# Mask through a product, exponential sums in PSUM and eight key blocks in a windowed attention kernel with two expert layers

## The chip, the cores and the metric

The kernel runs on one core of one Trainium2 chip. The core has TensorE (PE, with its weight loads shown apart as PEld), VectorE (DVE), ScalarE (ACT), GpSimd (POOL) and SyncE (SP), which here only issues DMAs. The metric is the device time of one execution in microseconds. Of the kernel before, three runs took 674.17, 674.81 and 678.31 us; their median is 674.81 us.

## The reference

There are three stages, all in float32.

- Attention: 4 batches, 8 heads, 512 local and 32 global tokens, head size 64. A local query sees the 32 global keys and the local keys at most 32 positions away (`mask = |i - j| <= 32`, else -1e9); a global query sees all 544 keys. Scores are scaled by 1/8; the softmax subtracts the row maximum and divides by (sum + 1e-9). This gives x of 2176 rows by 512.
- First layer: `h = x @ w_in` (512 to 1024); `solu = h * softmax(h)`; layer norm with `g_ln`; `@ w_out` (1024 to 512).
- Second layer: `h = x @ w_in` (512 to 2048); a piecewise square gate; `@ w_out` (2048 to 512).

The weights arrive as float64 and are converted on the chip to a high and a low float32 part.

## The kernel before

The local rows are cut into 16 tiles of 128 queries, four per batch, taken in the order SEQ = 0, 1, 3, 2, 4, 5, 7, 6 and so on; a number below is a place in this order. A tile has four chunks of 32 queries. Each chunk sees 128 keys: the chunk itself, one chunk on either side and the 32 global keys. So the scores of a tile are 8 heads by 128 keys for 128 partitions (4 heads by 32 queries), in two PSUM banks.

A step of a tile has a letter and its number t:

- q: the DMA of queries and keys (`load_qk`, `qkT`, two buffers); v: the DMA of the value windows (`load_vw`, `vw`, two buffers); w: the DMA of one of the first 16 pieces of the first layer's weights.
- S: 64 small products for the scores (L351), into one of two PSUM buffers of tag H, which the tiles of the first layer's `h` also use in turn. G: the products for the global queries (L404, L406); they read the same `qkT`.
- M: the mask on DVE (`mask`): an addition of `masks`, 128 x 512 values at the two edge blocks of every chunk, and, where a tile is the first or last of its batch, a memset of the missing block. R: the row maximum on DVE; Rn: its scaling.
- Ea, Eb: four exponentials each on ACT, one per head, with the row sum as accumulator output (L149, tile e). Ie: the addition of 1e-9 to the sums, on ACT where the list has a v behind it, else on DVE. I: their reciprocal on DVE.
- Ta, Tb: transposes on PE (`pPT`, L417); Pa, Pb: their copies to SBUF (`PT`). V: the products with the values (L432, tile o). X: their scaling on DVE (`xn`); XT: a transpose on DVE.
- A, C, B, D, F, H, L: the conversion of a weight piece (on DVE L173, L178, L180, L182, mostly).
- Z: three products with zeros (L276) that occupy PE in its first 20 us; ha to hB: the first layer's first product (L529); y, Y: its second (L270).

The order of all this is a written list, SCRIPT, whose 629 entries are issued one after the other; PE, SP, DVE, ACT and POOL keep its order on each engine. After it loops take over for the later tiles. A load waits on SP until its buffer is free, and all later loads wait behind it: q5 reuses the buffer of q3 and so waits for S3 and G3; v1 stands behind q5. The load w11 goes into the room of weight piece 3 and so waits for F3 on DVE; in SCRIPT F3 stands behind R5, D3 and X2, and on SP w14, q7, v4 and v5 stand behind w11.

The setup code (L125 to L130, L310) fills the identity, `masks` and `zero` on POOL and DVE. In DRAM, each tile's keys lie in 9 blocks of 32 (`KB`), where the blocks for global keys stand at 1, 4 and 7 (counted from 0), and a chunk's window starts at block 0, 2, 3 or 5 (`WSTART`).

Of the kernel before, what the change touches and what calls it, by code (L numbers as in the profile page):

```python
# [51 lines left out]
SCRIPT = """
Z0 q0 Z0 w0 qg0 S0 q1 w2 Z0 G0 w5 Gc0 S1 M0 A0v C0 R0 Rn0 B0 D0 F0 A2v Z0 G1 q2 M1 R1 C2 B2 D2 Ea0
A5 v0 Rn1 Z0 C5 B5 H0 Ta0 Eb0 F2 Ea1 Z0 Pa0 S2 Gc1 G2 Gc2 M2 Eb1 D5 H2 F5 R2 q3 L0v L2v Z0 Z0 G3
Gc3v Tb0 Ie0v w4 Rn2v I0 H5v Pb0 A4 C4 L5 V0 Ta1 Ea2 w1 S3 gm0 Pa1 A1v X0 Tb1 w7 Ie1v gn0 ge0 XT0 B4
q4 qg1 Eb2 xh0 C1 A7v gt0 B1 M3 C7 q5 xl0 D4 B7 Pb1 gp0 D1 R3 F1 D7 F4 v1 G4 n0 S4 w6 H4v M4 w3 Rn3v
Ie2v Ea3 Gc4 Ta2 Eb3 L4 V1 F7 H1 R4 I1 A6 Tb2 L1 H7 Pa2 S5 C6 Rn4v X1 v2 G5 Pb2 A3v L7 I2 XT1 q6 M5
B6 Ea4 Ta3 C3 B3 Gc5 Eb4 R5 V2 v3 Tb3 S6 Rn5v D3 Ie4v X2 Pa3 Pb3 F3 w9 D6 H3v w11 G6 Gc6v Ea5 M6
Ie3v Tb4 Eb5 F6 V3 I3 R6 w14 L3 XT2 A9v q7 H6 Ta4 X3 Pa4 L6 ha0 Rn6v v4 xh1 v5 A14 Ea6 C9 gi0 XT3 B9
hb0 Pb4 D9 hA0 Eb6 hB0 C14v B14 F9 G7 Ta5 Gc7 Tb5 V4 mx0 v6 D14 w8 ex0 F14 m9 Ie6v S7 ze0 I6 z0 I4  # L60
Pa5 u0 Pb5 M7 bn0v Ta6 xh2 pw0 X4 V5 Ie5v R7 Rn7v ha1 Ea7 gm1 Pa6 gn1 A11v XT4 Eb7 xl1 H9 Tb6 q8 I5
m14 C11 hb1 hA1 vn0 gc0 L9 w10 nn0v hB1 xl2v B11 ha2 xh3 D11 mx1 ta0 F11 X5 hb2 ex1 ge1 A8v hA2 hB2
H14v L14 ze1 tha0 z1 u1 tla0 Pb6 tb0 qg2 C8v m11 mx2 Ie7v V6 XT5 A10v bn1v thb0 gv0 pw1 S8 ex2 tlb0
X6 v7 go0 ze2v z2 u2 nn1v Ta7 w13 gt1 B8 Pa7 C10 I7 xh4 xl3 D8 ta1 gp1 B10 H11 F8 ha3 m8 L11 tha1 M8
v8 tb1 bn2v q9 Tb7 R8 thb1 H8 hb3 L8 hA3 Rn8v qg3 A13 D10 tlb1 w12 tla1 w15 Ea8 pw2 hB3 gc1 F10 XT6
mx3 s0 ya0 nn2 m10 Pb7 G8 Eb8 ex3 C13 B13 V7 Gc8 D13 X7 H10 ze3v G9 F13 z3 Gc9 S9 A12v Ie8v Ta8 L10
A15 u3 M9 bn3v R9 m13 xl4 C15 q10 Ya0 C12 tb2 B12 q11 ha4 s1 vn1 yca0 ta2 Pa8 hb4 Rn9 H13 thb2 hA4
D12 F12 Ea9 B15 m12 tha2 D15 hB4 tla2 tlb2 Tb8 F15 G10 L13 Eb9 A16 H12v Gc10v mx4 S10 I8 L12 M10 s2
Pb8 m15 G11 A17 XT7 v9 V8 pw3 Gc11 X8 v10 yb0 ex4 H15 ze4v C17 Ta9 L15v z4 Yb0 R10 Ie9v u4 xh5 nn3v
bn4v C16v I9 ycb0 Pa9v ta3 XT8 xl5 pw4 gm2 ha5 Rn10 tha3 tb3 hb5 nn4 B17 gi1 hA5 hB5 tla3 B16 Ea10  # L70
Eb10 thb3 Tb9 S11 xh6 Pb9 mx5 ex5 V9 ze5v tlb3 ta4 xh7 tha4v z5 u5 Ie10v A18 ya1 tb4 ha6 Ya1 v11 M11
bn5v hb6 X9 xl6v D16 D17 R11 F16 F17 hA6 gn2 yca1 Rn11 C18v H16v Ea11 tla4 Ta10 hB6 yb1 Eb11 thb4
tlb4 xh8v Tb10 q12 mx6 Pa10 B18 pw5 xl8 XT9 ge2 Pb10 I10 Ie11 D18 gv1 ex6 nn5v V10 ze6v X10 S12 Ta11
q13 z6 Yb1 M12 F18 go1 Pa11 u6 tb5 R12 ycb1 thb5v ha7 tlb5 gt2 L16 hb7 ta5 gp2 tha5 bn6 gc2 Tb11 I11
Rn12 xl7 pw6 H18v tla5 hB7 hA7 ya2 Ea12 nn6 Eb12 G12 Pb11v mx7 Gc12v S13 G13 ex7 gi2 Gc13v M13 Ie12v
v12 V11 q14 o0 tb6 thb6 L18 ze7 Ya2 ta6 z7 R13 Rn13v Ea13 Eb13 s3 xd0 u7 xd1 tlb6 XT10 H17v tha6
bn7v tla6 L17v Ie13 o1 X11 I12 I13 vn2 yca2 pw7 nn7 v13
"""
# [1203 lines left out]
```

## Time and profile before

| what | value |
|---|---|
| median of 3 runs | 674.81 us (674.17 to 678.31) |
| span of the profiled execution | 673.8 us; the page gives no other time for it |
| PE busy | 655.2 us (97%), 6089 instructions |
| PEld busy | 577.5 us (86%), 6092 |
| DVE busy | 432.9 us (64%) |
| ACT busy | 369.5 us (55%) |
| POOL busy | 259.8 us (39%) |
| DMA | 114.24 MB, 170 GB/s over the span |

A busy PE is not PE at its peak, because matmuls are pipelined and their ends are modelled. Idle time of an engine that nothing waits for costs nothing. In the page's 40 slices of 16.8 us each, PE's tenths are 7, 6, 8 and then 9 to the end but for the last slice.

### The profile page before, as it was taken

How to read it: one execution, taken by the hardware profiler on the slowest of the kernel's cores; microseconds unless marked ns; L12 is line 12 of the kernel's file. 1: busy time of each engine (PE TensorE's matmuls, PEld its weight loads, DVE VectorE, ACT ScalarE, POOL GpSimd, SP SyncE). 2: the span in 40 equal slices, each digit the busy share in tenths (PEclk: the TensorE clock that was granted, in tenths of full speed). 3: DMA queues.
4: the chain of work that ended last, by engine and by line, in shares of the span. 5: the costliest groups of instructions: out<-in, count | busy, mean ns of one | idle time of the engine just before them, and what ended most of it. 6: DMA issues, size and time to landing. Idle time of an engine off the chain costs nothing.

```text
span 673.8 us, 15103 instructions
## 1 busy us (share of the span) xinstructions
PE 655.2 (97%) x6089; PEld 577.5 (86%) x6092; DVE 432.9 (64%) x766; ACT 369.5 (55%) x918; POOL 259.8 (39%) x293
## 2 busy tenths in 40 slices
PE   7689999999999999999999999999999999999997
PEld 3467888989899889999999998998888888988986
DVE  5989987776787679654887679455655453333332
ACT  4888987556554244345666554554444466344443
POOL 2343463121112114203444676356776655222321
PEclk8979999999999999999999999999999999999999
DMA  8988854425752613301665341663333465744522
GB/s 321 358 348 333 343 203 159 165 65 164 288 193 92 254 32 125 95 1 32 187 188 186 128 125 63 217 220 126 125 126 125 134 210 190 237 136 157 170 81 80
DMA packets 29686, 114.24 MB, mean 170 GB/s; under 512 B 3376, under 2 KB 3888, under 8 KB 27056
## 3 DMA queue, kind: packets, MB, share of 16 engines
q1 hardware_dynamic: 29616, 113.28, 48.4%
q8 instruction: 48, 0.79, 0.5%
q14 instruction: 22, 0.18, 0.1%
HBM read 88.88 MB, written 24.38 MB: 168 GB/s over the span
## 4 chain that ended last, share of the span: by engine, by line
PE 90%; DMA 5%; DVE 3%; issue 1%; ACT 1%; SPq 0%; ACTq 0%
PE acc L270 26%; PE h L270 25%; PE yT L270 14%; PE h L529 13%; DMA vw<-in_vwin_dram 2%; PE plnT L594 2%; PE o L432 2%; DMA qkT<-in_qk_dram 2%; PE S L351 2%; PE pPT L417 2%; PE y L270 1%; PE og L492 1%; DVE xy L140 1%; PE G L404 0%; DVE w L180 0%
## 5 line engine op out<-in xcount | busy, mean ns | idle before, releaser
L270 PE MATMUL acc<-wo,g 128*128 128x512 f32 x816 | 211.3, 393 | 0.0
L270 PEld LDWEIGHTS acc<-wo,g 128*128 128x128 f32 x816 | 149.8, 188 | 23.2
L164 POOL TENSOR_TENSOR g<-xy,g 128x384 fp32r<-128x384 f32 (+1 forms) x65 | 62.8, 974 | 139.8 <-ACT g L149 122.4
L149 ACT ACTIVATE xy<-xy 128x384 f32<-128x384 f32 (+1 forms) x144 | 72.7, 505 | 71.5 <-DVE xy L140 68.5
L529 PE MATMUL h<-win,x 128*128 128x512 f32 x408 | 101.3, 400 | 0.0
L270 PE MATMUL yT<-lnT,wout 128*128 128x256 f32 x768 | 95.7, 284 | 0.0
L270 PEld LDWEIGHTS yT<-lnT,wout 128*128 128x128 f32 x768 | 93.4, 189 | 0.9
L529 PEld LDWEIGHTS h<-win,x 128*128 128x128 f32 x408 | 74.8, 188 | 15.9
L140 DVE TENSOR_TENSOR xy<-h,xy 128x384 f32<-128x384 f32 (+1 forms) x64 | 33.5, 524 | 62.1 <-PE h L270 60.9
L777 POOL TENSOR_TENSOR g<-xy,g 128x192 fp32r<-128x192 f32 x60 | 51.4, 876 | 54.2 <-ACT g L149 46.9
L149 ACT ACTIVATE g<-xy 128x384 fp32r<-128x384 f32 (+1 forms) x96 | 48.0, 500 | 18.7 <-DVE xy L140 16.7
L270 PE MATMUL h<-yT,w2i 128*128 128x384 f32 (+1 forms) x300 | 56.4, 334 | 0.0
L149 ACT ACTIVATE xy<-h 128x384 f32<-128x384 f32 (+1 forms) x64 | 30.0, 469 | 46.2 <-PE h L270 46.2
L270 PE MATMUL h<-yT,S 128*128 128x384 f32 (+1 forms) x288 | 54.9, 325 | 0.0
L270 PEld LDWEIGHTS h<-yT,w2i 128*128 128x128 f32 x300 | 52.5, 188 | 2.3
L140 DVE SCALAR_TENSOR_TENSOR xy<-h,xy 128x384 f32<-128x384 f32 (+1 forms) x48 | 26.1, 545 | 43.9 <-ACT xy L149 43.7
L270 PEld LDWEIGHTS h<-yT,S 128*128 128x128 f32 x288 | 48.8, 188 | 5.5 <-DVE xy L140 1.7
L149 ACT ACTIVATE e<-S,nm 128x128 f32<-128x128 f32 x128 | 45.3, 379 | 8.0 <-PE plnT L594 4.3
L571 POOL TENSOR_TENSOR rstd<-rstd,nhalf 128x1 f32<-128x1 f32 x17 | 11.4, 668 | 82.8 <-DVE rstd L140 49.6
L517 POOL TENSOR_TENSOR x<-xy,x 128x512 fp32r<-128x512 f32 x15 | 19.8, 1323 | 43.6 <-ACT x L149 35.5
L270 PE MATMUL h<-yT,lnT 128*128 128x384 f32 (+1 forms) x180 | 34.0, 334 | 0.1
L140 DVE SCALAR_TENSOR_TENSOR xy<-xy 128x384 f32<-128x384 f32 (+1 forms) x48 | 28.9, 602 | 7.8 <-ACT xy L149 7.8
(147 smaller groups left out, 1059.3 us busy)
## 6 DMA issues: line engine op xcount, KB each, us to landing
vw<-in_vwin_dram SPq DMA_DIRECT2D x16, 1024.0 KB, 7.0
wo<-w2d_o SPq DMA_DIRECT2D x32, 512.0 KB, 3.7
qkT<-in_qk_dram SPq DMA_DIRECT2D x15, 832.0 KB, 7.4
wraw<-in_w2i_dram SPq DMA_DIRECT2D x16, 512.0 KB, 3.7
wraw<-in_w2o_dram SPq DMA_DIRECT2D x16, 512.0 KB, 4.2
w2d_o<-wo SPq DMA_DIRECT2D x16, 512.0 KB, 5.1
w2d_s<-S SPq DMA_DIRECT2D x16, 512.0 KB, 5.5
S<-w2d_s SPq DMA_DIRECT2D x16, 512.0 KB, 5.9
```

The costliest lines, as they stand in the source:

```text
L140: self.last = getattr(nc.vector, name)(*args, **kw)
L149: vec.act = nc.scalar.activation(**kw)
L164: eng.tensor_tensor(out=lo, in0=src, in1=hi.bitcast(F32), op=ALU.subtract)
L270: mm(out=dst, lhsT=pairs[i][0][x], rhs=pairs[i][1][y], start=start and j == 0, stop=stop and j == 3 * n - 1, **kw)
L351: mm(out=S[32 * hp:32 * hp + 32, par, ci], lhsT=qT[r, hp, ci], rhs=kT[r, hp, w:w + 4].rearrange("p c d -> p (c d)"), start=True, stop=True)
L417: nc.tensor.transpose(ps[:, hp], eT[t][:, HP * par + hp], ident)
L432: mm(out=o[rows, ci, par], lhsT=PT[t][:, par, ci, rows], rhs=w[:, ci, D * h:D * h + D], start=True, stop=True)
L517: eng.tensor_tensor(out=xT[t][1], in0=x[:, :, n:n + P], in1=xT[t][0].bitcast(F32), op=ALU.subtract)
L529: mm(out=hps[t][:, half], lhsT=x[i][:, k], rhs=win[j][:, k, sl], start=not lo and j == 0 and k == 0, stop=lo and k == KD - 1)
L571: nc.gpsimd.tensor_tensor(sts[t].rstd, sts[t].rstd, nhalf, ALU.pow)
L594: nc.tensor.transpose(ps[:, k], ln[t][:, P * c:P * c + P], ident)
L777: eng.tensor_tensor(out=out, in0=x, in1=y, op=ALU.subtract)
```

## The change

The written list keeps its order but for two things: M1, M3 and M5 are gone, and each Ie stands directly behind the Eb of its tile instead of some way later.

- For tiles 0 to 5 the mask's addition on DVE is replaced by two products ahead of S, one for each PSUM bank: identity times a bfloat16 mask of 512 columns, with start and no stop, after which the 64 score products add to it. The memset of a missing block stays on DVE (tiles 0, 2 and 4).
- The accumulator output of an exponential goes to the first value of that head's scores in PSUM, which this exponential has read. Ie reads the eight sums there and writes them, with 1e-9 added, to SBUF. So the PSUM buffer is free only after Ie.
- Keys are stored in 8 blocks for 9: the global keys stand at blocks 2 and 5, the windows start at 0, 1, 3, 4. A load q has 768 KB for 832 KB. The windows keep the position of the masked blocks.
- Z reads 128 zeros four times for 512 zeros; POOL builds `maskb` and `identb` in the setup with a memset and five copies.

```diff
-WSTART = (0, 2, 3, 5)
-KB = 9
+WSTART = (0, 1, 3, 4)
+KB = 8
+MASKED = (0,1,2,3,4,5)
...
-            mm(out=ps, lhsT=zero[:, :P], rhs=zero, start=True, stop=True)
+            mm(out=ps, lhsT=zero, rhs=zero.unsqueeze(1).to_broadcast([P, 4, P]), start=True, stop=True)
...
-    zero = at1.tile([P, 512], BF16, name="zero")
+    zero = at1.tile([P, P], BF16, name="zero")
+    maskb = at1.tile([P, 4, 4, 32], BF16, name="maskb")
+    identb = at1.tile([P, P], BF16, name="identb")
...
+    nc.gpsimd.memset(maskb, 0.0)
+    nc.gpsimd.tensor_copy(identb, ident)
+    for c in range(4):
+        nc.gpsimd.tensor_copy(maskb[:, c, 0:4:3], masks)
...
+        own = t not in MASKED
+        for par in range(0 if own else 2):
+            mm(out=S[:, par].rearrange("p c n -> p (c n)"), lhsT=identb, rhs=maskb.rearrange("p c a n -> p (c a n)"), start=True, stop=False, skip_group_check=True)
...
-                       rhs=kT[r, hp, w:w + 4].rearrange("p c d -> p (c d)"), start=True, stop=True)
+                       rhs=kT[r, hp, w:w + 4].rearrange("p c d -> p (c d)"), start=own, stop=True, skip_group_check=not own)
...
-        tt(out=edge, in0=edge, in1=masks.unsqueeze(1).to_broadcast([P, H, 2, 32]), op=ALU.add)
+        if t not in MASKED:
+            tt(out=edge, in0=edge, in1=masks.unsqueeze(1).to_broadcast([P, H, 2, 32]), op=ALU.add)
...
-            act(out=eT[t][:, h], in_=heads(t)[:, h], func=AF.Exp, bias=nms[t][:, h:h + 1], scale=SCALE, accum_out=rs[t][:, h:h + 1])
+            act(out=eT[t][:, h], in_=heads(t)[:, h], func=AF.Exp, bias=nms[t][:, h:h + 1], scale=SCALE, accum_out=heads(t)[:, h, 0:1])
...
+    def sums_of(t):
+        return heads(t)[:, :, 0]
...
-        plus(rs[t])
+        plus(rs[t], of=sums_of(t))
...
-                        k = kT[r, hp, 2:8].rearrange("p (a c) d -> p a c d", a=2)[:, :, 0:2].rearrange("p a c d -> p a (c d)")
-                        mm(out=o[:, 32:32 + P].rearrange("p (a n) -> p a n", a=2), lhsT=lhsT, rhs=k, start=True, stop=True)
+                        k = kT[r, hp, 1:7].rearrange("p (a c) d -> p a c d", a=2)[:, :, 0:3:2]
+                        mm(out=o[:, 32:32 + P].rearrange("p (a c d) -> p a c d", a=2, c=2), lhsT=lhsT, rhs=k, start=True, stop=True)
...
-                plus(rs[i] if kind == "Ie" else sts[SEQ[i]].s, bool(v))
+                plus(rs[i] if kind == "Ie" else sts[SEQ[i]].s, bool(v), sums_of(i) if kind == "Ie" else None)
...
-        at = {0: -1, 2: 0, 3: 1, 5: 2, 6: 3, 8: 4}
+        at = {0: -1, 1: 0, 3: 1, 4: 2, 6: 3, 7: 4}
```

The weight step m also takes the engine that its caller names; in the list and the loops that is POOL, as before.

## Rows read from the trace of the kernel before

**Rows 1.** Stretch, length, busy PE, PEld, DVE, ACT, POOL (instructions), clock, DMA share, GB/s.
```profile
60.00:280.00 220.00, 219.88 (x2896) 196.35 (x2896) 173.81 (x321) 126.41 (x350) 64.99 (x61) 1.00 0.50 179
...
10.00:20.00 10.00, 8.61 (x177) 4.23 (x179) 8.66 (x16) 8.18 (x40) 1.23 (x2) 0.83 1.01 374
...
32.60:36.20 3.60, 1.11 (x62) 0.98 (x63) 3.10 (x6) 3.00 (x12) 2.87 (x3) 0.84 1.04 424
36.20:40.00 3.80, 3.80 (x95) 2.92 (x93) 2.29 (x5) 2.69 (x11) 2.12 (x3) 0.50 1.02 417
40.00:44.00 4.00, 4.00 (x145) 3.41 (x151) 4.00 (x8) 3.59 (x17) 0.00 (x0) 0.77 0.73 291
44.00:46.60 2.60, 2.39 (x100) 1.87 (x85) 2.51 (x7) 2.60 (x16) 1.29 (x1) 1.00 0.41 151
```

**Rows 2.** PE's waits from 0 to 80 us: total us, times, longest.
```profile
PE o L432 <- issue: 3.0, 2, 2.3
...
PE o L432 <- DMA vw<-in_vwin_dram: 1.5, 2, 0.8
```

**Rows 3.** Chain that ended last, 0 to 120 us: start us, us, what.
```profile
13.97 7.02 DMA qkT<-in_qk_dram
...
26.04 6.61 DMA vw<-in_vwin_dram
...
33.76 2.31 issue
...
42.78 0.60 DVE xn L140
43.38 0.61 DVE w L182
...
45.38 9.44 DMA vw<-in_vwin_dram
```

**Rows 4.** DMA issues, 0 to 60 us: count, KB each, median us to landing.
```profile
qkT<-in_qk_dram SPq DMA_DIRECT2D x8, 832.0 KB, 7.6
```

**Rows 5.** Timeline, POOL: start, us, instruction; and the costliest such group.
```profile
2.74 0.21 POOL L130 TENSOR_SCALAR_AFFINE_SELECT masks<-masks 32x32 f32<-32x32 f32 x1
...
masks.py:199 POOL TENSOR_SCALAR_AFFINE_SELECT ident<-ident 128x128 f32<-128x128 f32 x1 | 0.3, 293 | 0.0
```

**Rows 6.** Timeline, PE (Z at 15.26: first one, then all three).
```profile
10.42 1.44 PE L351 MATMUL S<-qkT 64*32 64x128 f32 x64 [1.52 <-DMA qkT<-in_qk_dram]
...
15.26 0.38 PE L276 MATMUL Z<-zero 128*128 128x512 bf16 x1
...
15.26 0.81 PE L276 MATMUL Z<-zero 128*128 128x512 bf16 x3
...
40.99 1.50 PE L432 MATMUL o<-vw,PT 128*32 128x64 f32 x64
...
54.96 1.10 PE L432 MATMUL o<-vw,PT 128*32 128x64 f32 x64 [0.83 <-DMA vw<-in_vwin_dram]
```

**Rows 7.** Timeline, DVE: start, us, instruction; in brackets the idle time before.
```profile
8.01 0.43 DVE L173 TENSOR_SCALAR w<-xy 128x512 int32<-128x512 int32 x1 [0.81 <-DMA xy<-in_w1i_dram]
...
36.69 0.69 DVE L140 TENSOR_TENSOR xn<-o,rs 128x512 f32<-128x512 f32 x1 [0.90 <-PE o L432]
...
39.69 0.70 DVE L140 TENSOR_TENSOR S<-S,masks 128x512 f32<-128x512 f32 x1 [1.02 <-PE S L351]
```

**Rows 8.** ACT groups, 0 to 60 us: count, busy us, mean ns, idle before.
```profile
L149 ACT ACTIVATE e<-S,nm 128x128 f32<-128x128 f32 x57 | 20.2, 376 | 0.7 <-DVE nm L140 0.4 <-DVE xn L140 0.3
L149 ACT ACTIVATION_READ_ACCUMULATOR e<-S,nm 128x1 f32 x56 | 12.1, 216 | 0.0
```

**Rows 9.** Stretches that end at the two stalls, and the page's instruction queue.
```profile
0.00:33.90 33.90, 23.88 (x601) 13.94 (x605) 25.48 (x48) 22.56 (x96) 9.86 (x25) 0.95 0.91 340
33.90:58.30 24.40, 20.97 (x509) 16.33 (x508) 22.26 (x45) 20.18 (x78) 8.05 (x9) 0.86 0.82 326
...
q8 instruction: 48, 0.79, 0.5%
```

More of the change, by code (lines that the diff above doesn't have):

```diff
@@ L50 @@
 SCRIPTED = 8
+MASKED = (0,1,2,3,4,5)
+PLAIN = ()
 SCRIPT = """
[L53 to L77, printed above, removed]
+Z0 q0 Z0 w0 qg0 S0 q1 w2 Z0 G0 w5 Gc0 S1 M0 A0v C0 R0 Rn0 B0 D0 F0 A2v Z0 G1 q2 R1 C2 B2 D2 Ea0
@@ new lines @@
+A5 v0 Rn1 Z0 C5 B5 H0 Ta0 Eb0 Ie0v F2 Ea1 Z0 Pa0 S2 Gc1 G2 Gc2 M2 Eb1 Ie1v D5 H2 F5 R2 q3 L0v
+L2v Z0 Z0 G3 Gc3v Tb0 w4 Rn2v I0 H5v Pb0 A4 C4 L5 V0 Ta1 Ea2 w1 S3 gm0 Pa1 A1v X0 Tb1 w7 gn0 ge0
+XT0 B4 q4 qg1 Eb2 Ie2v xh0 C1 A7v gt0 B1 C7 q5 xl0 D4 B7 Pb1 gp0 D1 R3 F1 D7 F4 v1 G4 n0 S4 w6
+H4v M4 w3 Rn3v Ea3 Gc4 Ta2 Eb3 Ie3v L4 V1 F7 H1 R4 I1 A6 Tb2 L1 H7 Pa2 S5 C6 Rn4v X1 v2 G5 Pb2
+A3v L7 I2 XT1 q6 B6 Ea4 Ta3 C3 B3 Gc5 Eb4 Ie4v R5 V2 v3 Tb3 S6 Rn5v D3 X2 Pa3 Pb3 F3 w9 D6 H3v
+w11 G6 Gc6v Ea5 M6 Tb4 Eb5 Ie5v F6 V3 I3 R6 w14 L3 XT2 A9v q7 H6 Ta4 X3 Pa4 L6 ha0 Rn6v v4 xh1
@@ new lines @@
+v5 A14 Ea6 C9 gi0 XT3 B9 hb0 Pb4 D9 hA0 Eb6 Ie6v hB0 C14v B14 F9 G7 Ta5 Gc7 Tb5 V4 mx0 v6 D14 w8
+ex0 F14 m9 S7 ze0 I6 z0 I4 Pa5 u0 Pb5 M7 bn0v Ta6 xh2 pw0 X4 V5 R7 Rn7v ha1 Ea7 gm1 Pa6 gn1 A11v
+XT4 Eb7 Ie7v xl1 H9 Tb6 q8 I5 m14 C11 hb1 hA1 vn0 gc0 L9 w10 nn0v hB1 xl2v B11 ha2 xh3 D11 mx1
+ta0 F11 X5 hb2 ex1 ge1 A8v hA2 hB2 H14v L14 ze1 tha0 z1 u1 tla0 Pb6 tb0 qg2 C8v m11 mx2 V6 XT5
+A10v bn1v thb0 gv0 pw1 S8 ex2 tlb0 X6 v7 go0 ze2v z2 u2 nn1v Ta7 w13 gt1 B8 Pa7 C10 I7 xh4 xl3
+D8 ta1 gp1 B10 H11 F8 ha3 m8 L11 tha1 M8 v8 tb1 bn2v q9 Tb7 R8 thb1 H8 hb3 L8 hA3 Rn8v qg3 A13
@@ new lines @@
+D10 tlb1 w12 tla1 w15 Ea8 pw2 hB3 gc1 F10 XT6 mx3 s0 ya0 nn2 m10 Pb7 G8 Eb8 Ie8v ex3 C13 B13 V7
+Gc8 D13 X7 H10 ze3v G9 F13 z3 Gc9 S9 A12v Ta8 L10 A15 u3 M9 bn3v R9 m13 xl4 C15 q10 Ya0 C12 tb2
+B12 q11 ha4 s1 vn1 yca0 ta2 Pa8 hb4 Rn9 H13 thb2 hA4 D12 F12 Ea9 B15 m12 tha2 D15 hB4 tla2 tlb2
+Tb8 F15 G10 L13 Eb9 Ie9v A16 H12v Gc10v mx4 S10 I8 L12 M10 s2 Pb8 m15 G11 A17 XT7 v9 V8 pw3 Gc11
+X8 v10 yb0 ex4 H15 ze4v C17 Ta9 L15v z4 Yb0 R10 u4 xh5 nn3v bn4v C16v I9 ycb0 Pa9v ta3 XT8 xl5
+pw4 gm2 ha5 Rn10 tha3 tb3 hb5 nn4 B17 gi1 hA5 hB5 tla3 B16 Ea10 Eb10 Ie10v thb3 Tb9 S11 xh6 Pb9
@@ new lines @@
+mx5 ex5 V9 ze5v tlb3 ta4 xh7 tha4v z5 u5 A18 ya1 tb4 ha6 Ya1 v11 M11 bn5v hb6 X9 xl6v D16 D17
+R11 F16 F17 hA6 gn2 yca1 Rn11 C18v H16v Ea11 tla4 Ta10 hB6 yb1 Eb11 Ie11 thb4 tlb4 xh8v Tb10 q12
+mx6 Pa10 B18 pw5 xl8 XT9 ge2 Pb10 I10 D18 gv1 ex6 nn5v V10 ze6v X10 S12 Ta11 q13 z6 Yb1 M12 F18
+go1 Pa11 u6 tb5 R12 ycb1 thb5v ha7 tlb5 gt2 L16 hb7 ta5 gp2 tha5 bn6 gc2 Tb11 I11 Rn12 xl7 pw6
+H18v tla5 hB7 hA7 ya2 Ea12 nn6 Eb12 Ie12v G12 Pb11v mx7 Gc12v S13 G13 ex7 gi2 Gc13v M13 v12 V11
+q14 o0 tb6 thb6 L18 ze7 Ya2 ta6 z7 R13 Rn13v Ea13 Eb13 Ie13 s3 xd0 u7 xd1 tlb6 XT10 H17v tha6
@@ L78 @@
+bn7v tla6 L17v o1 X11 I12 I13 vn2 yca2 pw7 nn7 v13
 """
@@ L183, in conv @@
         if step == "m" and w.scale is not None:
-            return nc.gpsimd.tensor_tensor(out=w.t3, in0=w.t3, in1=w.scale.unsqueeze(2).to_broadcast(list(w.t3.shape)), op=ALU.mult)
+            return eng.tensor_tensor(out=w.t3, in0=w.t3, in1=w.scale.unsqueeze(2).to_broadcast(list(w.t3.shape)), op=ALU.mult)
         if step == "H" and eng is nc.vector:
@@ L378, in exps, with plus @@
         for h in range(HP * half, HP * half + HP):
-            act(out=eT[t][:, h], in_=heads(t)[:, h], func=AF.Exp, bias=nms[t][:, h:h + 1], scale=SCALE, accum_out=rs[t][:, h:h + 1])
-    def plus(a, scalar=False):
+            act(out=eT[t][:, h], in_=heads(t)[:, h], func=AF.Exp, bias=nms[t][:, h:h + 1], scale=SCALE, accum_out=heads(t)[:, h, 0:1])
+    def plus(a, scalar=False, of=None):
         if scalar:
-            act(out=a, in_=a, func=AF.Copy, bias=EPS_SM)
+            act(out=a, in_=a if of is None else of, func=AF.Copy, bias=EPS_SM)
         else:
-            vec.tensor_scalar(a, a, EPS_SM, None, ALU.add)
+            vec.tensor_scalar(a, a if of is None else of, EPS_SM, None, ALU.add)
+    def sums_of(t):
+        return heads(t)[:, :, 0]
     def rsum(t):
-        plus(rs[t])
+        plus(rs[t], of=sums_of(t))
         vec.reciprocal(rs[t], rs[t])
```

## The prediction

> **What bounds the kernel now.** I read the busy time by stretch first. From 60 us to 280 us PE is busy for 219.88 of 220 us [rows 1], and the page's slices show it so to the end. What happens there on another engine is hidden as long as PE is fed, and the change adds nothing to PE there. So the change can move the end only by moving the moment, near 60 us, from which PE never waits again. All that follows is about the first 60 us.
>
> There the waits of PE come next [rows 2], then the chain of waits [rows 3]. The chain runs from load to load: q3 (issued 13.97, 7.02 us), then S3 frees the buffer for q5, and v1 behind it lands after 6.61 us; V1 stops in its middle for 2.31 us with no releaser ("issue"); then S5, R5, X2 and F3 on DVE let SP issue w11, w14, q7 and v4, and v4 takes 9.44 us from its issue at 45.38. V4 starts at 54.96 when it has landed [rows 6]. DVE is busy nearly throughout, yet it waits 0.90 us for V1 at X1 and 1.02 us for S5 at M5 [rows 7]: it isn't the chain by itself. DMA has share 1.01 to 1.04 between 10 and 20 us and between 32.6 and 40 us, and 0.73 and 0.41 after that [rows 1].
>
> **The change, part by part.** The sum is made against the profiled execution: span 673.8 us, 1.0 us under the median of the runs, 674.8; I add that 1.0 at the end.
>
> *Loads q.* Each has 64 KB less of 832 KB [rows 4]. By the time q3 lands, q0 to q3 have moved 256 KB less; at 374 GB/s [rows 1], with DMA full, that is 0.70 us. q5 saves 64 KB before v1, at 424 GB/s 0.15 us; q7 the same before v4. I take -0.70, -0.15 and -0.15; the bounds are 0 (if something other than bytes sets the landing) and these values.
>
> *Mask products.* The nearest row is Z, the same shape: three take 0.81 us at clock 1.00 [rows 6]. Two thirds of it, 0.54, is the upper bound; the first alone lasts 0.38, so each further one adds (0.81-0.38)/2 = 0.215, and a pair in a stream adds 0.43. I take 0.43, as S follows at once. Where the clock is 0.50 (1.2 GHz) I double it: 0.86. Tile by tile:
> - S0 also waits for POOL, whose last select ends at 2.95; six small operations of at most 0.293 us [rows 5] end by 4.7. With 0.43 and some 1.5 us for 64 products S0 ends by 6.7, and R0 stands behind a DVE conversion that starts at 8.01 when its weights land [rows 7]. Cost 0; cover left 1.3.
> - S1: PE waits 1.52 us for q1 [rows 6], and the two products need no keys. Cost 0. S2: it delays G2 and so q4 by up to 0.43, but q4 isn't on the chain. Cost 0.
> - S3 is on the chain: +0.43. S4 is followed by a wait of PE for v1 of 0.7 us (1.5 in two waits, the longer 0.8) [rows 2]. Cost 0.
> - S5 lies between 36.2 and 40 us, where the clock was 0.50 throughout, after PE had been busy 1.11 of 3.60 us [rows 1]: +0.86; lower bound 0.43.
>
> *Mask additions.* Six of 0.70 us [rows 7] leave DVE, 4.2 us. M0's and M1's room goes into waits for loads and S1. M2 to M4 are 2.1 us before X1, where DVE waits for V1 anyway: it waits longer. M5's goes into the wait for S5. So 0 on the chain, and what is late next is V1, S5, V2. If DVE were the chain, it would be up to -2.1; that is a rival.
>
> *Sums into PSUM.* The trace has no ACT output into PSUM. An exponential and its accumulator read last 376 and 216 ns [rows 8] and overlap. For the read into PSUM I bound the difference by half its duration either way, 0.1 us, so 0.8 us in eight; I take 0, the value of the row it is nearest to, the same read into SBUF. The last tile of the opening whose buffer PE then needs at once is 5; there up to 0.8 us would delay ha, and behind it PE has 0.83 us of wait before V4 [rows 6] as cover. The Trainium skill ("ScalarE: Activation LUTs", "What happens when an `exp` ACTIVATE runs") calls PSUM the lower-latency destination for ScalarE. By that the difference is a gain, and no run here shows it; the sum stays the same, as the cover stands at the same place.
>
> *Ie.* It now stands on ACT before what followed Eb, and holds the PSUM buffer for about 0.22 us more (the accumulator read, 0.216, is the nearest row). For ha, which takes tile 5's buffer, this is +0.22 on PE, before the same cover. Ie11 and Ie13 stand on DVE and wait there for ACT; behind them are conversions of a stretch in which DVE is busy 79% [rows 1] and PE needs nothing at once. Cost 0.
>
> *Z, the pattern of G, smaller `zero`.* The number of columns is the same. Cost 0.
>
> **The sum.** V1: -0.70 + 0.43 - 0.15 = -0.42. V2: -0.42 + 0.86 = +0.44. V2 ended at 40.99 + 1.50 = 42.49; now 42.93. X2 started at 42.78 [rows 3] behind D3, which comes earlier by M5's room; so X2 now waits for V2 and starts 0.15 later; F3 and w11 too. q7 gives back 0.15. v4 lands at the same time as before: 0.00. PE reaches V4 0.44 + 0.22 = 0.66 later than it did, within its 0.83. So the time is 673.8 + 0.0 + 1.0 = 674.8 us: no change that can be measured. Its own range, from the bounds, is 673.9 (mask of S5 at full clock and V2 no gate) to 675.8 (no gain from bytes); with the sums at their upper bound V4 would be 0.66 + 0.8 - 0.83 = 0.6 late, which lies within it.
>
> **The stall inside V1.** The term that I put at 0 and am least sure of. 1206 matmul and load records come before it and 1017 lie between it and the second one, of 0.7 us, in V5 [rows 9, 2]. TensorE's queue fetched 48 pieces in 0.79 MB [rows 9], 16 KB each; 12,181 PE and PEld instructions over 48 are 254, and 1017 is four times 254. So both stalls look like the ends of fetched pieces, with DMA full around the first [rows 1]. By V1 the change has put 20 instructions (four for each of S0 to S4) ahead: the piece now ends 20 instructions sooner in V1, still there. I take the same stall. The Trainium skill ("Runtime: NRT & Kernel Launch", "Instruction fetch mechanics") says that crossing a block is mostly hidden. By that rule the 2.31 us would not be there; the trace disagrees at two of the nine or so pieces in 60 us, so it can vanish as well as grow.
>
> **Rivals.**
> - *The fetch meets a pause of PE and the stall goes* (chance 18%). 2.31 us less for V1; S5 then runs at full clock, and DVE has its 2.1 us. What is late next is DMA: between 40 and 46.6 us it is idle for (1-0.73)*4.0 + (1-0.41)*2.6 = 2.6 us [rows 1], and the loads up to v4 can't come earlier than that. 674.8 - 2.6 = 672.2; with the second stall gone too 671.5. For it: seven pieces ended without a stall. Against: V1 is the densest run of instructions.
> - *DVE was the chain* (12%): the M2 to M4 part passes through, 674.8 - 2.1 = 672.7. For it: DVE busy 4.00 of 4.00 us before F3 [rows 1]. Against: its waits at X1 and M5 [rows 7].
> - *Slower: the bytes give nothing and the products cost* (16%). If the landings don't follow the bytes, S3 and S5 remain: V2 ends at 42.49 + 1.29 = 43.78, X2, F3 and v4 are 1.00 later: 675.8. It decides from the point where q3 takes more than 6.8 us from issue to landing.
> - *The stall grows or a third one comes* (8%): another 2.31 us in the densest part, with DMA full: 677.1.
> - *The sums or Z don't do what is written*: the read takes as long into PSUM, Z's repeated zeros run like plain ones. Both are my zeros already, so this is part of the forecast.
>
> My forecast has 40%; 6% are left to what the trace doesn't hint at, half of it on either side and over 1%.
>
> **How the numbers follow.** Predicted is the forecast's 674.8. Range 671.3 to 677.3: it takes in all four rivals and leaves out the last 6% and a part of the bounds. 1% is 6.7 us, about what a measurement of this kernel can tell from no change; none of the cases reaches it, up to 58 us PE is idle for 10.0 + 3.4 us in all [rows 9], half of which would have to go, so faster by over 1% gets 0.05, slower 0.05, within 0.90.
>
> **What would show it.** In the profile after: DMA of q3 at about 6.5 us from its issue; pairs of mask products of 0.43 us before S3 and up to 0.86 before S5; no DVE addition on S before tile 6; X1 waiting longer than 0.90 us for V1; a stall of some 2 us in V1, about ten products sooner; V4 starting within 1 us of 54.96. Wrong it would be if V4 starts 2 us earlier with the stall gone, if PE waits for ACT's Ie ahead of an S or ha after 60 us, or if PE isn't full after 60 us.

## The result: slower, outside the range, and the profile after

The changed kernel takes 681.56 us (median of four runs, 680.47 to 683.34) against 674.97 for the kernel before in the same comparison: the medians are 6.6 us apart. The ratio is 1.0088, with a 95% interval of 1.0061 to 1.0115; it is formed from the single runs of a comparison and isn't the quotient of the medians (of 675 us it is 5.9). The range ended at 677.3. The profiled execution of the changed kernel is the slowest of its four; its span is 681.3 us, before's was 673.8, so the two traces are 7.5 us apart.

One row holds most of it. The waits of PE in the changed kernel, over the whole span (total us, times, longest):

```profile
PE h L545 <- DVE rs L143: 4.0, 1, 4.0
...
PE G L420 <- issue: 1.8, 1, 1.8
...
PE o L448 <- issue: 0.9, 2, 0.6
```

The first row wasn't there before: PE waited 4.0 us for `rs` on DVE, in a part of the span where I had said it never waits. The timeline of PE in the changed kernel shows where (start, us, instruction; in brackets the idle time before and its releaser):

```profile
161.07 0.60 PE L610 MATMUL plnT<-ident,e 128*128 128x128 f32 x4
165.68 7.40 PE L545 MATMUL h<-win,x 128*128 128x512 f32 x24 [4.01 <-DVE rs L143]
```

It is the first product of the first layer for one tile, 24 products. Before, the same rows were:

```profile
159.40 0.60 PE L594 MATMUL plnT<-ident,e 128*128 128x128 f32 x4
159.76 5.85 PE L529 MATMUL h<-win,x 128*128 128x512 f32 x24
```

So 1.67 us of the 7.5 had come up by `plnT`, and 5.80 came at this one h: it starts 4.25 later against `plnT`, and its 24 products take 7.40 for 5.85, 1.55 more. The other executions below say which of the two parts is the change. From the start of this `plnT` to the end of its span before's takes 514.4 us (673.8 less 159.40). The ten others in which PE doesn't wait at this h take 513.9 to 515.3; the changed kernel takes 520.2, 5.8 more than before's. The start of `plnT` scatters: e1, e8 and e8b run the same steps as the changed kernel up to there, and have it at 158.85, 159.07 and 160.14, where the changed kernel has 161.07 and before's 159.40. So the 5.80 at h is the change, and the 1.67 is no more than that scatter.

What DVE did at that place in the changed kernel:

```profile
157.96 1.21 DVE L143 TENSOR_REDUCE nm<-S 128x8 f32<-128x1024 f32 x1
165.45 0.17 DVE L143 TENSOR_SCALAR rs<-S 128x8 f32<-128x8 f32 x1 [6.29 <-ACT e L152]
...
165.76 1.24 DVE L143 SCALAR_TENSOR_TENSOR e<-e,s,h 128x1024 f32<-128x1024 f32 x1
```

The second row is Ie13. It stands 6.29 us, idle, until ScalarE has finished the last tile's exponentials. Behind it in DVE's order stands u7 (the last row, `hmul`), which reads the h of the tile before and so frees its PSUM buffer. In the kernel before, u7 ran early and Ie13 (`rs`) late:

```profile
157.63 1.24 DVE L140 SCALAR_TENSOR_TENSOR e<-e,s,h 128x1024 f32<-128x1024 f32 x1
...
164.74 0.17 DVE L140 TENSOR_SCALAR rs<-rs 128x8 f32<-128x8 f32 x1
```

The two buffers of tag H are held by that h, until u7, and by the scores S13, until Ie13 has read the sums in them. Both now end at or behind Ie13, and the next h starts at 165.68, when Ie13 has run.

The starts also tell which buffer it takes. Before, h starts at 159.76, behind u7 and ahead of S13's exponentials (from 160.10): it has the buffer that u7 freed. In the changed kernel it starts ahead of u7 (165.76), released by Ie13: it has S13's own. The built programs say the same. That choice isn't the cost: u7 now ends at 167.00, so the other buffer would have come later still.

Ahead of this stands ScalarE. Its timeline in the changed kernel, from the first to the last of the eight exponentials of S13:

```profile
161.76 0.37 ACT L152 ACTIVATE e<-S,nm 128x128 f32<-128x128 f32 x1 [2.36 <-PE plnT L610]
162.03 0.16 ACT L152 ACTIVATION_READ_ACCUMULATOR e<-S,nm 128x1 f32 x1
...
165.26 0.16 ACT L152 ACTIVATION_READ_ACCUMULATOR e<-S,nm 128x1 f32 x1
```

The first of them starts when PE has done `plnT` (161.67), which reads a tile e; the trace names it as the releaser. So PE's last product ends, ScalarE then runs eight exponentials, DVE Ie13, and only then PE goes on.

The pitch of these exponentials is the second finding. Before, in the timeline of ScalarE, one started every 0.345 us:

```profile
10.17 0.36 ACT L149 ACTIVATE e<-S,nm 128x128 f32<-128x128 f32 x1
10.42 0.20 ACT L149 ACTIVATION_READ_ACCUMULATOR e<-S,nm 128x1 f32 x1
10.52 0.36 ACT L149 ACTIVATE e<-S,nm 128x128 f32<-128x128 f32 x1
```

and in the changed kernel every 0.46 us:

```profile
11.12 0.37 ACT L152 ACTIVATE e<-S,nm 128x128 f32<-128x128 f32 x1
11.39 0.16 ACT L152 ACTIVATION_READ_ACCUMULATOR e<-S,nm 128x1 f32 x1
11.58 0.37 ACT L152 ACTIVATE e<-S,nm 128x128 f32<-128x128 f32 x1
```

Each instruction by itself became shorter. The groups of ScalarE from 0 to 60 us in the changed kernel (count, busy us, mean ns) answer to [rows 8]:

```profile
L152 ACT ACTIVATE e<-S,nm 128x128 f32<-128x128 f32 x56 | 20.6, 367 | 1.4
L152 ACT ACTIVATION_READ_ACCUMULATOR e<-S,nm 128x1 f32 x56 | 9.3, 166 | 0.0
```

The read takes 166 ns for 216. But the next exponential used to start 0.10 after the read had begun, beside it; now it starts 0.19 after, when the read is over. A group's mean can't show that; the starts do.

Last, the clock. Stretches of the changed kernel (length; busy PE, PEld, DVE, ACT, POOL with instructions; granted clock, DMA share, GB/s):

```profile
161.70:165.70 4.00, 0.03 (x1) 0.03 (x1) 0.25 (x2) 3.71 (x17) 0.00 (x0) 1.00 0.24 66
165.70:173.00 7.30, 7.30 (x25) 5.81 (x26) 6.31 (x14) 2.37 (x6) 0.55 (x1) 0.77 0.43 136
...
167.70:168.70 1.00, 1.00 (x4) 0.81 (x3) 1.00 (x4) 0.97 (x4) 0.00 (x0) 0.50 0.00 0
```

PE was busy 0.03 of 4.00 us. In the stretch behind that the mean granted clock is 0.77; from 166.7 to 169.7 it is 0.50, which is 1.2 GHz, as in the last row. Three us at half speed cost about 1.5 (an estimate from these rows), which is the 1.55 us.

### The profile page after: what moved, and what is told of

It reads as the page before. It is cut to its first block, busy times and chain, and to the rows that moved or that the text cites. A ratio compares the mean times of both kernels' runs of the same rounds, so it can differ in the third digit from the quotient of the medians.

```text
span 681.3 us, 15118 instructions
## 1 busy us (share of the span) xinstructions
PE 661.2 (97%) x6099; PEld 580.7 (85%) x6104; DVE 427.2 (63%) x760; ACT 376.1 (55%) x918; POOL 261.5 (38%) x299
## 4 chain that ended last, share of the span: by engine, by line
PE 91%; ACT 4%; DVE 3%; issue 1%; POOL 0%; POOLq 0%; ACTq 0%
PE acc L273 26%; PE h L273 25%; PE h L545 14%; PE yT L273 13%; PE o L448 2%; PE plnT L610 2%; PE S L363 2%; ACT e L152 2%; PE pPT L433 2%; PE y L273 1%; PE og L508 1%; PE G L420 1%; DVE xy L143 1%; ACT Sg L152 0%; PE pg L488 0%
## 5 line engine op out<-in xcount | busy, mean ns | idle before, releaser
L545 PE MATMUL h<-win,x 128*128 128x512 f32 x408 | 103.0, 405 | 4.0 <-DVE rs L143 4.0
L545 PEld LDWEIGHTS h<-win,x 128*128 128x128 f32 x408 | 76.2, 192 | 20.5 <-DVE rs L143 4.2
L152 ACT ACTIVATE e<-S,nm 128x128 f32<-128x128 f32 x128 | 47.0, 368 | 10.2 <-PE plnT L610 3.8
L273 PEld LDWEIGHTS h<-yT,lnT 128*128 128x128 f32 x180 | 31.6, 188 | 2.0 <-DVE xy L143 0.5
```

The costliest lines, as they stand in the source:

```text
L152: vec.act = nc.scalar.activation(**kw)
L273: mm(out=dst, lhsT=pairs[i][0][x], rhs=pairs[i][1][y], start=start and j == 0, stop=stop and j == 3 * n - 1, **kw)
L545: mm(out=hps[t][:, half], lhsT=x[i][:, k], rhs=win[j][:, k, sl], start=not lo and j == 0 and k == 0, stop=lo and k == KD - 1)
```

## The experiments

The theory after the two traces: Ie13's place on DVE costs most of it, the sums in PSUM some, and the mask products with the eight blocks nothing. The rivals: the mask products or blocks are what costs; h waits for S13's own buffer, wherever Ie13 stands.

| kernel | median us | ratio to before (95%) |
|---|---|---|
| changed | 681.56 | 1.0088 (1.0061 to 1.0115) |
| e1 Ie13 on ScalarE | 677.45 | 1.0031 (1.0016 to 1.0045) |
| e2 sums in SBUF | 679.61 | 1.0077 (1.0059 to 1.0094) |
| e3 mask products and blocks alone | 674.27 | 1.0001 (0.9981 to 1.0022) |
| e4 before, Ie13 moved | 680.07 | 1.0077 (1.0047 to 1.0107) |
| e5 blocks alone | 674.88 | 0.9987 (0.9975 to 0.9999) |
| e6 mask products alone | 675.92 | 1.0007 (0.9994 to 1.0021) |
| e7 sums in the other bank | 676.06 | 1.0024 (1.0003 to 1.0044) |
| e8 Ie13 behind u7 | 676.23 | 1.0007 (0.9995 to 1.0020) |
| e8b the same again | 676.19 | 1.0018 (1.0002 to 1.0034) |
| e9 e8, sums in SBUF | 675.41 | 1.0009 (0.9992 to 1.0026) |
| e10 sums alternating | 677.25 | one run |
| e11 sums without own wait | 675.79 | 1.0021 (1.0005 to 1.0037) |

Before's median was 674.84 beside e1 to e4, 675.43 beside e5 to e8, 675.18 beside e8b to e10 and 674.71 beside e11; ratios, not times, are compared across these groups. A ratio of 0.001 is 0.7 us.

**e1, Ie13 on ScalarE** (the changed kernel):

```diff
- ... Eb13 Ie13 s3 xd0 u7 xd1 ...
+ ... Eb13 Ie13v s3 xd0 u7 xd1 ...
```

> The changed kernel with one entry different: Ie13 runs on ACT and no longer on DVE. Theory A (two costs: DVE stands at Ie13 for 6.3 us, so u7 behind it frees no buffer and TensorE idles 4.0 us and then runs 1.5 us longer at the lower clock; the rest, 1.7 us, comes from the exponentials before 60 us): the wait of 4.0 us is gone, 681.6 - 5.8 = 675.8 us, with TensorE still about 1.7 us late at 60 us. Theory B (it is the PSUM buffer of tile 13 that is held longer, whichever engine adds): the wait stays, 681 us.

The wait is gone: `plnT` at 158.85 is followed by h at 159.20. The ratio falls from 1.0088 to 1.0031, so theory A holds for the larger part. It missed the rest: 677.45 is 1.7 us over what it gave, and PE isn't 1.7 us late near 60 us, as V4 starts at 55.03, where before's started at 54.96. Where the remaining 0.0031 (2.1 us) goes isn't shown.

**e2, sums in SBUF** (the changed kernel, Ie where the change put it, now adding in place):

```diff
- accum_out=heads(t)[:, h, 0:1]
+ accum_out=rs[t][:, h:h + 1]
```

> The changed kernel with the exponentials' sums going to SBUF again and Ie adding in place; list, mask products and eight blocks stay. Theory A: an exponential with its accumulator read is back from a pitch of 0.46 to 0.345 us, TensorE reaches its last wait near 60 us some 1.7 us earlier, and the exponentials of tile 13 end 0.9 us earlier, so the wait at Ie13 is 3.1 instead of 4.0 us: 679.0 us. Theory C (the mask products or the loads cost the 1.7 us): pitch back, but the opening as slow: 680.7 us.

The waits of PE:

```profile
PE h L545 <- ACT e L152: 3.1, 1, 3.1
```

The same h still waits, now 3.1 us and for the last exponential itself, as S13's buffer is then free when Eb13 ends. 4.01 - 3.06 = 0.95, and eight exponentials at 0.115 more make 0.92: that much of the wait was the pitch. The time, 679.61, lies between theory A's 679.0 and theory C's 680.7 and doesn't decide between them; e3 does.

**e3, mask products and blocks alone** (sums in SBUF, every Ie in its place of before):

> Mask products and eight key blocks alone: sums in SBUF and every Ie where the kernel before has it. Theory A: neither cost is left, 674 to 675 us, at most 1 us from the kernel before. Theory C: 676.5 us.

1.0001 (0.9981 to 1.0022): these two parts together cost nothing that can be measured, with about 1.4 us of room either way. The rival falls.

**e4, only Ie13 moved** (the kernel before, otherwise untouched):

```diff
- ... Eb13 s3 xd0 u7 xd1 ... L17v Ie13 o1 ...
+ ... Eb13 Ie13 s3 xd0 u7 xd1 ... L17v o1 ...
```

> The kernel before with one entry moved: Ie13, on DVE and with sums in SBUF, directly behind Eb13. Theory A: DVE waits there for ACT, u7 is late, TensorE idles about 3.1 us and runs on at the lower clock for a while: 675.0 + 4.5 = 679.5 us. Theory B: sums in SBUF hold no PSUM buffer, so 675.0 us.

One word of the list makes the kernel before 1.0077 times as long, 5.2 us (3.2 to 7.2). Its timeline of DVE:

```profile
161.69 0.17 DVE L140 TENSOR_SCALAR rs<-rs 128x8 f32<-128x8 f32 x1 [5.54 <-ACT e L149]
...
162.00 1.24 DVE L140 SCALAR_TENSOR_TENSOR e<-e,s,h 128x1024 f32<-128x1024 f32 x1
```

and of PE:

```profile
158.06 0.60 PE L594 MATMUL plnT<-ident,e 128*128 128x128 f32 x4
161.71 5.84 PE L529 MATMUL h<-win,x 128*128 128x512 f32 x24 [3.06 <-ACT e L149]
```

The same picture with no other part of the change in it: DVE stands 5.54 us, u7 runs at 162.00 for 157.63, PE idles 3.06 us. Here too h starts ahead of u7, released by S13's last exponential, as with the sums in SBUF nothing else holds that buffer. The profiled execution is the fastest of the four (677.48 us) and takes 3.2 us more than before's from `plnT` to the end; what the slower three lost besides isn't in a trace.

**e8, Ie13 behind u7, still on DVE** (the changed kernel):

```diff
- ... Eb13 Ie13 s3 xd0 u7 xd1 ...
+ ... Eb13 s3 xd0 u7 Ie13 xd1 ...
```

> The changed kernel with the one step Ie13 (adding the epsilon to the last tile's sums) moved in the list from ahead of s3, xd0 and u7 to directly behind u7, still on DVE. Theory A (the loss is only that DVE stands at Ie13 for ScalarE's sums with u7, which frees the PSUM buffer of h, behind it): TensorE's wait of 4.0 us ahead of tile 8's h goes, and with it the lower clock behind it, so 676 to 678, like Ie13 on ScalarE (677.45). Rival B (the wait is for the scores' own PSUM buffer, which Ie13 holds wherever it stands): h starts late as now, 681. Rival C: the wait shortens to 1 or 2 us, 679.

It was run twice, 1.0007 and 1.0018; the second time beside e9, of which more below:

> Once more the changed kernel with Ie13 behind u7 and the sums still in PSUM, beside the run with the sums in SBUF, so that the two differ in the sums alone. Theory A (0.115 us per exponential in the tiles where ScalarE is the chain): 1.5 to 2.5 us longer than that run, 676 to 677. Rival B (ScalarE is covered, the sums cost nothing once Ie13 is out of the way): equal to it within 0.5 us.

The timeline of DVE in the second run:

```profile
158.38 1.24 DVE L143 SCALAR_TENSOR_TENSOR e<-e,s,h 128x1024 f32<-128x1024 f32 x1
...
164.54 0.17 DVE L143 TENSOR_SCALAR rs<-S 128x8 f32<-128x8 f32 x1 [4.91 <-ACT e L152]
```

and of PE:

```profile
160.14 0.60 PE L610 MATMUL plnT<-ident,e 128*128 128x128 f32 x4
160.50 5.82 PE L545 MATMUL h<-win,x 128*128 128x512 f32 x24
```

Ie13 still makes DVE stand, for 4.91 us, but u7 is ahead of it and PE goes on at once, at full clock. So the length of DVE's wait isn't what costs; what stands behind it is. Moving one step past three takes the ratio from 1.0088 to 1.0007 and 1.0018. The rival falls as it was put, that h waits for S13's buffer wherever Ie13 stands: here it takes the other one, while S13's exponentials still run. Only with u7 behind Ie13 is S13's buffer the first to come free, and then PE does wait for it.

**e9, both causes undone** (e8 with the edit of e2):

> The changed kernel with both suspected causes taken away and all else kept (mask products, 8 blocks, the early places of Ie on DVE or ScalarE): Ie13 stands behind u7, and the sums of exponentials go to SBUF. Theory A (two causes, 5 us for Ie13 and 2 for the sums in PSUM, and nothing else): 674 to 675, ratio 0.998 to 1.001, as the mask products and blocks with the old places of Ie gave (674.27). Rival B (the early places of the other Ie steps cost too): 676 or more.

675.41, ratio 1.0009 and not told apart from before: nothing else in the change shows a cost, the early places of the other Ie steps included (the interval leaves room for up to 1.8 us). Against e8b in the same comparison the sums in PSUM cost 0.8 us by the medians, and the two intervals overlap. These 0.8 lie between the theory's 1.5 to 2.5 and the rival's nothing: outside the stall at Ie13 the cost of the sums isn't shown.

**e5, blocks alone, and e6, mask products alone** (the kernel before with one part each):

```diff
- WSTART = (0, 2, 3, 5)
- KB = 9
+ WSTART = (0, 1, 3, 4)
+ KB = 8
```

> The kernel before with nothing changed but the keys in 8 blocks for 9 (smaller moves of q's piece and of G's operand, no mask products, sums of exponentials in SBUF, the places of all steps as before). Theory A (the terms of the prediction): three shorter loads, -0.70, -0.15 and -0.15, so about 673.8 against the 674.8 of before, ratio 0.9985. Rival B (TensorE is not waiting for bytes at these places): 674.8, ratio 1.000. C (the saved bytes move a later stall on): 676 or more.

> The kernel before with the first six tiles' mask written by two products ahead of the scores, DVE's addition left out for them; 9 blocks, sums in SBUF, places of all other steps as before. Theory A (the terms of the prediction): the products lie on TensorE's path in tiles 3 and 5, +0.43 and +0.86, and DVE's M was hidden, so about 676.1, ratio 1.002. Rival B (DVE's mask was on the chain of the opening): six masks of about 0.5 us come off it, 672 to 674, ratio below 0.999. With the two alone and both together on record, their sum can be compared with the run that had both (1.0001 with -0.0019 to +0.0021).

e5: 0.9987, -0.9 us (-1.7 to -0.1), where the terms gave -1.00. It is the only version here whose interval lies below 1, and only just (0.9999). e6: 1.0007, +0.5 us (-0.4 to +1.4), where they gave +1.29. So the rival of e6 (the masks were on DVE's chain) falls, and the terms' sum, +0.29, is what e3 can't tell from nothing.

**e7, e10 and e11: why the next exponential waits.** All three have Ie13 on ScalarE, as e1. In e7 the second half's sums went into the bank that its exponentials don't read:

```diff
- accum_out=heads(t)[:, h, 0:1]
+ accum_out=heads(t)[:, h % HP, half:half + 1]
```

> The changed kernel with Ie13 on ScalarE, and with the sums of the second half's four exponentials (heads 4 to 7, which read the second PSUM bank of the scores) written into the first bank; the first half's stay in the bank that its exponentials read. Theory A (the next exponential waits for the accumulator's read only because it reads the bank that is being written): pitch 0.46 us within the first half as now, 0.345 within the second, and the opening about 0.4 us per tile shorter, 676.5 to 677. Rival B (any PSUM destination of the accumulator holds the next exponential back): 0.46 in both halves, 677.5. Rival C (the tile as a whole is what is tracked: a semaphore between neighbours): 0.46 in both halves and a wait in the trace.

The timeline of ScalarE in e7, the second half of tile 0:

```profile
13.98 0.37 ACT L152 ACTIVATE e<-S,nm 128x128 f32<-128x128 f32 x1
...
14.45 0.37 ACT L152 ACTIVATE e<-S,nm 128x128 f32<-128x128 f32 x1
```

0.47, and 0.46 from there to the next: the bank isn't it. In e10 every second sum went to SBUF (`accum_out=rs[t][:, h:h + 1] if h % 2 else heads(t)[:, h, 0:1]`):

> The changed kernel with Ie13 on ScalarE; the sums of heads 0, 2, 4, 6 go to PSUM and those of heads 1, 3, 5, 7 to SBUF (these four lack the epsilon). It asks what holds the next exponential back. Theory A (it waits until the accumulator's read has written PSUM): 0.46 us from an even head to the next odd one, 0.345 from an odd to the next even. Rival B (an exponential whose own sum goes to PSUM starts late): the reverse, 0.345 from even to odd and 0.46 from odd to even. Rival C (PSUM anywhere in the group): 0.46 throughout. Time of A or B: about 676.

```profile
11.08 0.37 ACT L152 ACTIVATE e<-S,nm 128x128 f32<-128x128 f32 x1
...
11.57 0.37 ACT L152 ACTIVATE e<-S,nm 128x128 f32<-128x128 f32 x1
...
12.03 0.37 ACT L152 ACTIVATE e<-S,nm 128x128 f32<-128x128 f32 x1
```

In this timeline of ScalarE in e10 the pitch is 0.49 from odd to even and 0.46 from even to odd: neither A nor B, and close to C's numbers. But even a sum into SBUF was waited for, and that pointed away from the memory and to the program. In the list of ScalarE's built instructions, with the semaphores that each waits for, the changed kernel has, for the first half of tile 0,

```
L152 ACTIVATE e,S<-S,nm 128x128 [waits DVE_49]
L152 ACTIVATE e,S<-S,nm 128x128 [waits Activation_49] x3
```

and the kernel before

```
L149 ACTIVATE e,rs<-S,nm 128x128 [waits DVE_49]
L149 ACTIVATE e,rs<-S,nm 128x128 x3
```

`Activation_49` is ScalarE's own semaphore: each exponential waits until the one before it has finished. The sum is written into the tile S that the next one reads, so the language layer orders the two. e11 separates this wait from PSUM (shortened here to tiles 3 to 5; in tiles 6 and 7 the sums go into spare columns of the tile `nm`; the step gc0 stands earlier, so that the PSUM buffer is free):

```diff
+ own[t] = psY.tile([P, 512], F32, tag="Y", name="own")        # tiles 3 to 5
...
- accum_out=heads(t)[:, h, 0:1]
+ accum_out=rs[t][:, h:h + 1] if h >= HP and h % 2 else own[t][:, h:h + 1]
```

> In the built program of the changed kernel each exponential that follows another of its tile waits for a semaphore of ScalarE itself, set by the exponential before it: the language layer orders instructions that write and read one PSUM tile. Here (Ie13 on ScalarE) tiles 3 to 5 put their sums elsewhere: the first half's into a PSUM tile of their own, where each still waits for the one before; in the second half heads 4 and 6 into that PSUM tile and heads 5 and 7 into SBUF, so that none waits for its neighbour. Tiles 6 and 7 put them into SBUF, into the tile that holds the bias that the next exponential reads (no such wait in the program). Theory A (the semaphore wait is what costs, not PSUM): 0.46 us in the first half, about 0.345 in the second half of tiles 3 to 5, after PSUM and after SBUF sums alike, and 0.345 in tiles 6 and 7. Rival B (PSUM as the destination of a sum): 0.46 from heads 4 and 6 to the next, 0.345 from head 5 to 6. Time, three tiles half and two wholly freed: 675.5 to 677.

Tile 3 in the timeline of ScalarE of e11, first half (each waits for the one before) and then heads 4 to 6 (none waits for its neighbour):

```profile
31.54 0.37 ACT L152 ACTIVATE e<-S,nm 128x128 f32<-128x128 f32 x1
31.80 0.16 ACT L152 ACTIVATION_READ_ACCUMULATOR e<-S,nm 128x1 f32 x1
32.00 0.37 ACT L152 ACTIVATE e<-S,nm 128x128 f32<-128x128 f32 x1
...
33.18 0.38 ACT L152 ACTIVATE e<-S,nm 128x128 f32<-128x128 f32 x1
33.43 0.19 ACT L152 ACTIVATION_READ_ACCUMULATOR e<-S,nm 128x1 f32 x1
33.48 0.40 ACT L152 ACTIVATE e<-S,nm 128x128 f32<-128x128 f32 x1
33.73 0.24 ACT L152 ACTIVATION_READ_ACCUMULATOR e<-S,nm 128x1 f32 x1
33.82 0.40 ACT L152 ACTIVATE e<-S,nm 128x128 f32<-128x128 f32 x1
```

0.46 with the wait; without it 0.30 behind a sum in PSUM (33.18 to 33.48) and 0.34 behind one in SBUF (33.48 to 33.82). Tiles 4 and 5 show 0.30 to 0.32 and 0.34, and tiles 6 and 7 0.34. Theory A is shown for the pitch: with the sum in PSUM the semaphore costs 0.16 us, the destination by itself gains 0.04, and 0.115 is left. It had the same pitch behind either destination, which is wrong by those 0.04. In the time of the whole kernel the freed tiles show nothing: e11 (1.0021) can't be told from e1 (1.0031) or e7 (1.0024).

## Why the prediction was wrong

**The failed step: "Ie11 and Ie13 stand on DVE and wait there for ACT; behind them are conversions of a stretch in which DVE is busy 79% [rows 1] and PE needs nothing at once. Cost 0."** I put a wait into an in-order engine and took what stands behind it from an average, a busy share from 60 to 280 us. The list says what stands there: `Ie13 s3 xd0 u7`. u7 frees the buffer that PE's next h took at once; behind a waiting Ie13 it can't, and the only other buffer is held by the very exponentials that Ie13 waits for. Ie13 measured by itself costs 5.2 us (e4), and its removal gave 4.6 us with the sums in SBUF on either side (ratio 1.0077 in e2, 1.0009 in e9: 0.0068 of 675). For Ie11 the zero holds: PE has no wait at it. The last part of the prediction named a near relative among the signs of being wrong ("if PE waits for ACT's Ie ahead of an S or ha after 60 us"), but gave it no price and no chance. That sign itself didn't come: in the waits of the changed kernel PE waits for an Ie on ScalarE at S2 (0.70 us) and S6 (0.38), both before 60 us.

It could have been priced from before's rows. PE starts h at 159.76, right behind `plnT`. The exponentials of S13 need `plnT`'s end, so eight of them at 0.345, 2.8 us, lie between `plnT` and Ie13, and u7 behind that: PE would idle about 2.8 us at least (3.06 in e4).

**"From which PE never waits again"** was right of the kernel before and wrong as a frame. A stretch at 219.88 of 220 us busy [rows 1] has no idle time to lose, but a new wait in it went to the end in full: 4.01 us of wait and 1.55 of lower clock are nearly all of the 5.8 us between `plnT` and the end. I took "PE is full" to mean that nothing there could matter.

**Sums into PSUM: bound 0.1 us, taken as 0.** The measured term is +0.115 per exponential, just outside the bound, and it came from where I didn't look: not from the read (166 ns for 216) but from the overlap that a semaphore takes away. My rows gave both durations; "and overlap" was a fact of the program of before, not of the instruction. At Ie13 it made 0.95 of the 4.01 us; elsewhere e8b against e9 leaves 0.8 us that the intervals don't separate from nothing. The page "ScalarE: Activation LUTs" of the Trainium skill ("Step-by-step: what each stage is for") calls PSUM the lower-latency destination, and the trace of e11 agrees: without the wait the pitch is 0.30 behind a sum in PSUM and 0.34 behind one in SBUF.

**Loads: -1.00 in all; measured -0.9 (-1.7 to -0.1) in e5.** Right within the interval. The median from issue to landing of the loads of queries and keys, from 0 to 60 us (KB each, us), went from 7.6 [rows 4] to

```profile
qkT<-in_qk_dram SPq DMA_DIRECT2D x8, 768.0 KB, 6.9
```

The sign that I named for it failed, though: q3 was to take about 6.5 us from its issue, and over 6.8 would speak for the rival in which the bytes give nothing. It took 7.0 in the changed kernel and 7.2 in e5, for 7.02. It was issued earlier, at 13.09 and 12.22 for 13.97, and so landed earlier all the same. The saving lies in when the loads start, not in how long this one takes.

**Mask products: +1.29; measured +0.5 (-0.4 to +1.4) in e6.** Right within the interval. The pair ahead of S3 takes 0.31 at the timeline of PE in the changed kernel, the pair ahead of S5 from 38.51 to 39.03, 0.52:

```profile
4.65 1.01 PE L357 MATMUL S<-maskb,identb 128*128 128x512 bf16 x2 [0.72 <-POOL maskb L319]
5.59 2.81 PE L363 MATMUL S<-qkT 64*32 64x128 f32 x64
...
23.69 0.38 PE L357 MATMUL S<-maskb,identb 128*128 128x512 bf16 x1
24.00 1.16 PE L363 MATMUL S<-qkT 64*32 64x128 f32 x64
...
37.55 0.53 PE L448 MATMUL o<-vw,PT 128*32 128x64 f32 x19 [0.59 <-issue]
38.51 0.38 PE L357 MATMUL S<-maskb,identb 128*128 128x512 bf16 x1
```

I had 0.43 and 0.86; at S5 I had counted on the lower clock (0.50 before [rows 1]), and it wasn't there: its 64 products took 1.16 us for 1.96. S0 did wait for POOL, 0.72 us, and ended at 8.40, not by 6.7.

**Mask additions and X1.** As predicted: X1 waits 1.47 us for V1, where it waited 0.90 [rows 7].

**The stall inside V1.** Right in its place, wrong in its size. Before, V1 stopped with 10 of its 64 products left; in the changed kernel it stops with 19 left (the row at 37.55), nine products sooner, where I had said about ten. The stop is 0.59 us for 2.31, and there is a new one at G. In the timeline of PE before,

```profile
36.07 0.58 PE L432 MATMUL o<-vw,PT 128*32 128x64 f32 x10 [2.31 <-issue]
```

and in that of the changed kernel

```profile
46.48 0.38 PE L420 MATMUL G<-qkT,qkg 64*32 64x128 f32 x2 [1.79 <-issue]
```

With the second in V ("o", 0.9 in two) the changed kernel has 2.7 us of them, for 3.0 [rows 2]. In the waits of e3, e5 and e9 the stalls at V and G add up to 3.4, 2.3 and 3.8 us. Their places aren't chance. In e2, e3, e6, e7, e8, e8b, e9 and e10 V1 also stops with 19 products left, for 1.0 to 2.0 us; in e4 and e5, without the mask products, with 10 left, as before. From that stop to the next one of half a us or more in V or G lie 254 or 255 records of PE and PEld or about twice that (254 in e2, 509 in the changed kernel), and in the kernel before 1017. So the count of 254 in the prediction holds for where PE can stop. Whether it stops there, and for how long, differs from one execution to the next, and that the stop is a fetch is still only argued. What the stalls cost isn't settled: the ratios of e3, e5 and e9, 1.0001, 0.9987 and 1.0009, have intervals that overlap.

**V4 within 1 us of 54.96.** Wrong in the changed kernel's trace, 57.51, but e1, e8 and e8b run the same steps up to there and have 55.03, 55.35 and 56.08. One trace can't carry a forecast of 1 us at this place.

The rivals didn't hold either: all were about the first 60 us. The two on the slower side, 675.8 and 677.1, had the wrong mechanism.

## What to carry to other kernels

Before you move a step that waits, read the next few steps of the same engine's order and ask of each what buffer it frees and who needs it; an engine's busy share over a long stretch doesn't answer that. Where the bound engine has no idle time a new wait goes to the end in full, as here, so that is where to look, not only where it already waits. And when an output moves into a tile that the next instruction reads, look in the built program for a wait that wasn't there: compare starts, not durations. Before you explain a difference of one or two us at some place by the change, see how far that place moves between executions of the same steps: here it was 2.5 us at V4.
